# Value products of two units issued as one burst: second batch, first tokens, of an attention + MLP kernel

## The chip, the cores and the metric

The kernel runs on one core of a Trainium2 chip. The time is the device time of one launch in microseconds (us), taken as the median of several runs. Less is better.

## The reference

For 8 batches of 8 heads, 576 positions and head size 64, the reference computes causal windowed attention: heads 0 to 3 see the last 32 keys, heads 4 to 7 see every fourth of the last 128 keys ("dilated"). The result, laid out as 4608 tokens by 512 features, goes through a two-layer MLP:

```
scores = where(mask, q @ k.T / sqrt(64), -1e9)
attn   = exp(scores - max); attn = attn / (sum(attn) + 1e-9)
x      = (attn @ v) as (4608, 512)
h      = x @ w_in                # 512 -> 2048
out    = max(0.01 * h, h) @ w_out   # 2048 -> 512
```

All inputs and the output are float32; the kernel computes in fp16 and accumulates in float32.

## The kernel before

**Tiling.** Batches are taken in pairs, `m = b // 2`. Each batch has four *visits*, in the order `hp` = 2, 3, 0, 1: a visit is a pair of heads (2 and 3 are dilated, 0 and 1 plain). Batches 0 and 1 (`b < EARLY`) are cut in two parts. Part 0 takes 384 of the 576 positions in two units, `u` = 0 and 1; part 1 takes the rest in one unit. So part 0 of batch 1 is four visits of two units each.

**One unit** (function `unit`) is this chain. TensorE: scores of 128 keys against 384 query columns into the PSUM bank `sps` (L666 adds a bias that does the masking, L685 multiplies). ScalarE: the exponential into `ee` (L691). TensorE: value products into a PSUM bank `ops`. ScalarE: logarithm (L761) and then exponential with scale -1 (L763) of the sums, which gives their reciprocal in `rc`. VectorE: the product `ops * rc` into `xt` (L767), the normalisation. In part 0 of batches 0 and 1 (`TILED`) the value products are *half-width*: six matmuls per unit whose outputs have 64 partitions, 0 to 63 for one head of the pair and 64 to 127 for the other; four (L729) multiply by values, two (L717) by ones, for the sums.

**Buffers.** For this part there are two `ops` banks and one `sps` bank, given out in rings (`ring`), unit after unit. A unit's value products wait (`o_old`) for the normalisation of the unit that had the bank two units ago. `ee` has four buffers, `rc` three.

**The MLP.** Positions are taken in chunks of 384. For each chunk, `up` makes 16 groups of four matmuls with `w_in` (L792, 128 x 384, banks `hps`), ScalarE applies the leaky ReLU (L803), and `down` multiplies with `w_out` in three tiles of four *parts* of four matmuls each (L841, 128 x 512, banks `fps`); VectorE copies a finished tile out (L851). Chunk 0 is part 0 of batch 0, chunk 1 is part 0 of batch 1. Each `up` of chunk 1 needs the normalisations of all four visits of part 0 of batch 1 (`x_done[1, 0]`); the last visit, `hp` = 1, comes last. A tile of `down` needs one of two `fps` banks, so the third tile of a chunk starts when the first is copied out. The part p of `down` also needs its four slices of `w_out`, which are loaded and cast during this stage.

**What sets the order.** `_Plan.add` collects tasks with an engine, an assumed duration and latency, dependencies, a priority (small is urgent) and a `soft` time. `_Plan.run` goes through simulated time and gives each engine that is free a task whose dependencies are done; the order so found is the order of the instructions, and on the chip each engine takes its instructions in this order. Its choice is

```
pick = min(((t.ready + t.soft > at + 1e-9, t.prio, t.n), t)
           for t in could if t.ready <= at + 1e-9)
```

So a task with `soft` 0.4 (scores and value products) that has become ready less than 0.4 us ago yields to every other ready task that has waited long enough, whatever the priorities. The priorities near the change are: scores `first + step*n + 0.1` and values `first + step*n + 0.2` with first 20 and step 2 for part 0 of batch 1 (n counts visits); part 1 from 40; `up` of chunk 1 from 20.8 in steps of 1.3; parts of `down` of chunk 0 from 21.4 in steps of 1.73; the transposes of the last positions (`rest`, L557) 40. The assumed costs are 0.36 us for a unit's half-width value products and 0.25 latency after them; 0.06 + 0.00085 n and 0.1 + 0.00085 n for logarithm and exponential of n = 192 columns, 0.2 latency each; 0.38 and 0.2 latency for the normalisation; 0.865 for a part of `down`; 0.335 for the scores with their bias. Idle gaps that the plan sees are filled with dummy matmuls (L934), but only up to the first part of `down`.

Of the kernel before, what the change touches and what calls it, by code (L numbers as in the profile page):

```python
# [11 lines left out]
AF = mybir.ActivationFunctionType  # L12
ALU = mybir.AluOpType
# [47 lines left out]
class _Plan:  # L61
# [5 lines left out]
    def add(self, eng, dur, lat, deps, fn, prio, soft=0.0, kind=""):  # L67
        choices = eng if isinstance(eng, tuple) else ((eng, dur),)
        t = _Task(choices, lat, deps, fn, prio, soft, len(self.tasks), kind)
        self.tasks.append(t)  # L70
        return t
# [66 lines left out]
def kernel(  # L138
# [10 lines left out]
    nc = tc.nc  # L149
# [12 lines left out]
    EARLY = 2  # L162
# [14 lines left out]
    def at(tl, p0, p1, off, *dims):  # L177

        row = tl.ap[0][0]
        return bass.AP(tensor=tl.tensor, offset=tl.offset + p0 * row + off,  # L180
                       ap=[[row, p1 - p0]] + [list(d) for d in dims])
# [43 lines left out]
    add = plan.add  # L225
# [31 lines left out]
    def ring(name, n, users):  # L257

        r = rings.setdefault(name, [])
        waits = r[-n] if len(r) >= n else []  # L260
        r.append(users)
        return (len(r) - 1) % n, waits
# [39 lines left out]
    def heads_of(b, vi):  # L302
        return (2 * vi, 2 * vi + 1) if b < EARLY else (4 * (vi // 2) + vi % 2,
                                                       4 * (vi // 2) + vi % 2 + 2)
# [155 lines left out]
    def chunk_at(m, x):  # L460
        return next(c for c, (mc, xc, n) in enumerate(chunks) if mc == m and xc <= x < xc + n)

    def pieces(b, hp, u, tiled):


        dil = hp >= 2
        m, res = b // 2, []
        u_lo, u_hi = ((0, 96) if u < 2 else (96, 144)) if dil else (48 * u, 48 * u + 48)
        h0, h1 = heads_of(b, hp)
        xm = xt[m % 2]  # L470
        for u0, nu, base in segs[b]:
            lo, hi = max(u0, u_lo), min(u0 + nu, u_hi)
            if lo >= hi:
                continue
            key = (chunk_at(m, base), b % 2 if b < EARLY and lo >= 96 else 0)
            n = hi - lo
            x = base + lo - u0 + (2 * u * nu if dil and u < 2 else 0)
            xs = [[24, 2], [nu, 4], [1, 24]] if not dil else [[nu, 2 if u < 2 else 4], [1, n]]
            if tiled:
                cs = ([[96, 2], [24, 4], [1, 24]] if not dil else  # L480
                      [[192 // xs[0][1], xs[0][1]], [1, n]])
                res.append((key, 0, 128, at(xm, 0, 128, h0 // 2 * 1152 + x, *xs), 0, cs))
                continue
            step = 192 if not dil or u < 2 else 96
            cs = [[192, 2], [24, 4], [1, 24]] if not dil else [[step, xs[0][1]], [1, n]]
            if dil and b >= EARLY:
                p0 = h0 % 2 * 64
                res.append((key, 0, 64,
                            at(xm, p0, p0 + 64, h0 // 2 * 1152 + x, xs[0], [1152, 2], xs[1]), 0,
                            [cs[0], [step // 2, 2], cs[1]]))  # L490
                continue
            for hh, h in enumerate((h0, h1)):
                p0 = h % 2 * 64
                res.append((key, 0, 64, at(xm, p0, p0 + 64, h // 2 * 1152 + x, *xs),
                            step // 2 * hh, cs))
        return res


    x_done, x_free = {}, {1: w_used[14] + w_used[15]}
    k_turned = []  # L500
    rings["F"] = [[], k_turned]
# [136 lines left out]
    def unit(b, hp, part, u, turned, prio):  # L638
        dil = hp >= 2
        ready, t_users, qb, kb = turned  # L640
        na, c_qk, n_users, vt, v_deps, v_users = visits[b, hp, part]
        m, par = divmod(b, 2)
        tiled = (b, part) in TILED
        sk, ok = ("S0", "O0") if b == 0 and part == 0 else ("S", "O")
        sn, s_old = ring(sk, len(banks[sk]), s_users := [])
        on, o_old = ring(ok, len(banks[ok]), o_users := [])
        en, e_old = ring("E", NE, e_users := [])
        rn, r_old = ring("R", NR, r_users := [])
        st, ot, et, rt = banks[sk][sn], banks[ok][on], ee[en], rc[rn]
# [3 lines left out]
        small = dil and u == 2  # L653
# [3 lines left out]
        def scores(e):  # L657
# [18 lines left out]
            for i in range(2):  # L676
# [5 lines left out]
                else:  # L682
# [9 lines left out]
                                                 scale=SCALE), prio + 0.1)  # L692
        s_users.append(t_e)

        def mask(e):
# [11 lines left out]
        t_m = t_e if by_pe else add(  # L707
            (("DVE", 0.41), ("POOL", 0.95)) if b in POOL_MASK else "DVE", 0.41, 0.15, [t_e, t_con],
            mask, prio + 0.1)

        def values(e):
            if tiled:
                for x in range(5 if small else 3):
                    for hh in range(2):
                        p0 = 64 * hh
                        if x == (4 if small else 2):
                            nc.tensor.matmul(  # L717
                                ot[p0:p0 + 64, 192:384], ones,
                                (at(et, 0, 128, 48 * hh, [96, 4], [1, 48]) if small else
                                 at(et, 0, 128, 96 * hh, [192, 2], [1, 96])),  # L720
                                start=True, stop=True)
                        elif small:
                            nc.tensor.matmul(
                                ot[p0:p0 + 64, 48 * x:48 * x + 48],
                                at(vt, 0, 128, (hh * 8 + x) * 128, [1, D]),
                                et[:, 96 * x + 48 * hh:96 * x + 48 * hh + 48],
                                start=True, stop=True)
                        else:
                            nc.tensor.matmul(  # L729
                                ot[p0:p0 + 64, 96 * x:96 * x + 96],  # L730
                                at(vt, 0, 128, (hh * (8 if dil else 6) + 2 * u + x) * 128, [1, D]),
                                et[:, 192 * x + 96 * hh:192 * x + 96 * hh + 96],
                                start=True, stop=True)
                return
            if small:
                for s in range(4):
                    for hh in range(2):
                        c = 96 * s + 48 * hh
                        nc.tensor.matmul(  # L739
                            ot[:, c:c + 48],  # L740
                            at(vt, 0, 128, (hh * 8 + 4 * (b >= EARLY) + s) * 128, [1, 128]),
                            et[:, c:c + 48], start=True, stop=True)
                return
            for i in range(2):
                t = 2 * u + i
                for hh in range(2):
                    va = at(vt, 0, 128, (hh * (8 if dil else 6) + t) * 128, [1, 128])
                    c = 192 * i + 96 * hh
                    nc.tensor.matmul(ot[:, c:c + 96], va, et[:, c:c + 96],  # L749
                                     start=True, stop=True)  # L750

        t_v = add("PE", 0.36 if tiled else 0.21 if small else 0.17, 0.25, [t_m] + v_deps + o_old,
                  values, prio + 0.2, 0.4, "v")
        e_users.append(t_v)
        v_users.append(t_v)
        if tiled:
            r_in, r_out, n_r = ot[:, 192:384], rt[:, 0:192], 192
        else:
            r_in, r_out, n_r = ot[64:128, 0:384], rt[0:64, :], 384
        t_l = add("ACT", 0.06 + n_r * 0.00085, 0.2, [t_v] + r_old,  # L760
                  lambda e: nc.scalar.activation(out=r_out, in_=r_in, func=AF.Ln), prio + 0.2)  # L761
        t_r = add("ACT", 0.1 + n_r * 0.00085, 0.2, [t_l],
                  lambda e: nc.scalar.activation(out=r_out, in_=r_out, func=AF.Exp, scale=-1.0),  # L763
                  prio + 0.2)
        for key, p0, p1, dst, c, i_ in pieces(b, hp, u, tiled):
            def norm(e, p0=p0, p1=p1, dst=dst, c=c, i_=i_):
                nc.vector.tensor_tensor(out=dst, in0=at(ot, p0, p1, c, *i_),  # L767
                                        in1=at(rt, p0, p1, c, *i_), op=ALU.mult)
            t_n = add("DVE", 0.61 if dil and b >= EARLY else 0.38, 0.2,
                      [t_r] + x_free.get(m, []), norm, prio + 0.2)  # L770
            x_done.setdefault(key, []).append(t_n)
            o_users.append(t_n)
            r_users.append(t_n)


    gt_free = {1 - NG: sum(w_used[11:14], []), 2 - NG: w_used[0] + w_used[1]}
# [208 lines left out]
```

The softmax here doesn't subtract the row's maximum and nothing guards it: scores larger than these inputs give would overflow.

## Time and profile before

| | |
|---|---|
| median of 5 runs | 316.75 us (316.04 to 317.94) |
| the profiled execution | 317.94 us, its span in the profile 316.2 us |
| TensorE (PE) busy | 304.1 us, 96% of the span |
| ScalarE (ACT) busy | 219.4 us, 69% |
| VectorE (DVE) busy | 175.5 us, 56% |
| GpSimd (POOL) busy | 120.1 us, 38% |
| granted TensorE clock | 1.00 |
| value products of part 0 of batch 1 | start 43.15 us, last start 54.55 us |
| first `up` of chunk 1 | starts 56.92 us |

Rows of the groups and of the timeline name a line of the kernel (L792), the engine, the operation, and output and input by the program's names. In the timeline, columns are the start, the length from the first start to the last end, and a count of merged instructions. Ends of matmuls are modelled and overlap the next starts, so differences of starts are used here.

### The profile page before, as it was taken

The page shows a single profiled execution, that of the slowest core. Times are in us where ns is not written, and L with a number is a line of the kernel's source. Part 1 is how long each engine was busy: PE and PEld are TensorE (multiplying, and loading weights), DVE is VectorE, ACT ScalarE, POOL GpSimd, SP SyncE. Part 2 cuts the span into 40 slices and gives each one's busy share as a digit, 9 for nine tenths or more (in the row PEclk, how much of TensorE's full clock was granted, in tenths as well). Part 3 has the DMA queues.
Part 4 walks back from the last instruction along what each step waited for, and adds up shares of the span by engine and source line. Part 5 has one row for each costly group of instructions (what it writes and reads, how often), then busy time and mean ns, then how long its engine had stood idle before and what let it go on. Part 6 is the DMA issues. An engine that isn't in the chain of part 4 may idle for free.

```text
span 316.2 us, 6332 instructions
## 1 busy us (share of the span) xinstructions
PE 304.1 (96%) x2257; PEld 179.5 (57%) x2257; DVE 175.5 (56%) x396; ACT 219.4 (69%) x501; POOL 120.1 (38%) x174
## 2 busy tenths in 40 slices
PE   7858899999999999999999999999999999999995
PEld 3525554667777666655555555555555555555544
DVE  5855985647897776876758767664343421000011
ACT  3826585689898999988788888788787843333310
POOL 4457655382684545837628456450000000000000
PEclk9999999999999999999999999999999999999999
DMA  7999998999999899889989979711111111211113
GB/s 245 279 343 403 401 332 172 245 165 220 229 185 190 150 253 188 162 208 218 188 200 191 194 178 184 171 35 33 35 33 35 33 35 36 56 42 35 33 33 100
DMA packets 158175, 51.14 MB, mean 162 GB/s; under 512 B 139200, under 2 KB 151616, under 8 KB 158144
## 3 DMA queue, kind: packets, MB, share of 16 engines
q1 hardware_dynamic: 157696, 50.46, 67.1%
q10 hardware_dynamic: 448, 0.29, 0.4%
q8 instruction: 17, 0.28, 0.4%
q14 instruction: 14, 0.11, 0.1%
HBM read 41.30 MB, written 9.44 MB: 160 GB/s over the span
## 4 chain that ended last, share of the span: by engine, by line
PE 86%; DMA 4%; SPq 3%; DVE 3%; ACT 2%; issue 1%; POOL 0%; POOLq 0%
PE fps L841 39%; PE hps L792 37%; PE sps L685 4%; PE ops L749 3%; SPq L239 3%; DMA stg<-in_k_dram 2%; DMA stg<-in_q_dram 2%; DVE slots L509 1%; PE tp L557 1%; PE ops L739 1%; ACT gt L803 1%; PE sps L669 1%; DVE nat L249 1%; ACT rc L761 0%; PE sps L666 0%
## 5 line engine op out<-in xcount | busy, mean ns | idle before, releaser
L792 PE MATMUL hps<-xt,w_in 128*128 128x384 f16 (+1 forms) x824 | 149.9, 314 | 3.5 <-DVE w_in L249 1.4
L841 PE MATMUL fps<-w_out,gt 128*128 128x512 f16 (+1 forms) x592 | 145.7, 373 | 0.0
L803 ACT ACTIVATE gt<-hps 128x384 f16<-128x384 f32 (+1 forms) x206 | 93.9, 462 | 50.9 <-PE hps L792 46.9
L792 PEld LDWEIGHTS <-w_in 128*128 128x128 f16 x832 | 75.9, 98 | 46.8 <-DVE w_in L249 2.9
L841 PEld LDWEIGHTS <-gt 128*128 128x128 f16 x592 | 55.7, 98 | 45.1
L767 DVE TENSOR_TENSOR xt<-ops,rc 64x192 f16<-64x192 f32 (+2 forms) x138 | 52.3, 398 | 37.2 <-ACT rc L763 36.1
L544 POOL COPY slots<-turned 64x576 f16<-64x576 f16 x48 | 34.7, 723 | 59.8 <-DVE turned L539 57.3
L851 DVE COPY osb<-fps 128x512 f32<-128x512 f32 (+1 forms) x37 | 24.8, 670 | 55.7 <-PE fps L841 55.3
L705 DVE TENSOR_TENSOR ee<-ee,con 128x384 f16<-128x384 f16 x78 | 38.4, 495 | 30.5 <-ACT ee L691 29.8
L761 ACT ACTIVATE rc<-ops 64x384 f32<-64x384 f32 (+1 forms) x94 | 43.2, 463 | 14.5 <-PE ops L717 4.8
L691 ACT ACTIVATE ee<-sps 128x384 f16<-128x384 f32 x92 | 44.7, 486 | 10.3 <-PE sps L685 8.0
L763 ACT ACTIVATE rc<-rc 64x384 f32<-64x384 f32 (+1 forms) x96 | 46.8, 492 | 1.4
L249 POOL CAST nat<-stg 128x576 f16<-128x576 f32 (+1 forms) x52 | 35.0, 695 | 5.8 <-DMA stg<-in_k_dram 2.3
L685 PE MATMUL sps<-slots 128*128 128x192 f16 x152 | 25.0, 246 | 0.5 <-DVE slots L509 0.4
L685 PEld LDWEIGHTS <-slots 128*128 128x128 f16 x160 | 15.8, 102 | 11.7 <-DVE slots L509 0.8
L249 POOL CAST vd<-vst 128x1024 f16<-128x1024 f32 (+2 forms) x20 | 17.5, 897 | 6.3 <-DMA vst<-in_v_dram 6.1
L550 DVE STREAM_TRANSPOSE slots<-nat 128x576 f16<-128x576 f16 x24 | 18.0, 762 | 1.3 <-POOL nat L249 1.1
L539 DVE STREAM_TRANSPOSE turned<-nat 128x576 f16<-128x576 f16 x24 | 18.1, 763 | 0.1
L509 DVE COPY slots<-tp 64x128 f16<-64x128 f16 (+5 forms) x47 | 14.4, 319 | 4.8 <-PE tp L557 4.2
L749 PEld LDWEIGHTS <-vp 128*128 128x128 f16 x160 | 11.1, 98 | 5.6
L249 POOL CAST vp<-vst 128x768 f16<-128x768 f32 x16 | 12.9, 823 | 3.2 <-DMA vst<-in_v_dram 1.8
L749 PE MATMUL ops<-ee,vp 128*128 128x96 f16 x160 | 13.3, 206 | 0.0
(64 smaller groups left out, 132.6 us busy)
## 6 DMA issues: line engine op xcount, KB each, us to landing
vst<-in_v_dram SPq DMA_DIRECT2D x14, 512.0 KB, 5.1
stg<-in_q_dram SPq DMA_DIRECT2D x48, 144.0 KB, 4.1
stg<-in_k_dram SPq DMA_DIRECT2D x48, 144.0 KB, 3.0
vst<-in_v_dram SPq DMA_DIRECT2D x6, 768.0 KB, 5.7
out_dram<-osb SPq DMA_DIRECT2D x16, 192.0 KB, 2.3
gt<-in_moe_w_in_dram SPq DMA_DIRECT2D x5, 512.0 KB, 7.1
out_dram<-osb SPq DMA_DIRECT2D x24, 96.0 KB, 2.1
out_dram<-osb SPq DMA_DIRECT2D x14, 128.0 KB, 2.7
```

What stands on the lines that cost most here:

```text
L249: ENG[e].tensor_copy(out=dst, in_=src)
L544: lambda e, p0=p0, hh=hh: nc.gpsimd.tensor_copy(out=at(qb, p0, p0 + 64, hh * S + o, *od), in_=at(xb, p0, p0 + 64, i, *id_)), prio)
L685: nc.tensor.matmul(st[:, 192 * i:192 * i + 192], ka, qa, start=not by_pe, stop=i == 1 or not by_pe)
L691: lambda e: nc.scalar.activation(out=et, in_=st[:, 0:384], func=AF.Exp, scale=SCALE), prio + 0.1)
L705: ENG[e].tensor_tensor(out=io, in0=io, in1=mk, op=ALU.mult)
L749: nc.tensor.matmul(ot[:, c:c + 96], va, et[:, c:c + 96], start=True, stop=True)
L761: lambda e: nc.scalar.activation(out=r_out, in_=r_in, func=AF.Ln), prio + 0.2)
L763: lambda e: nc.scalar.activation(out=r_out, in_=r_out, func=AF.Exp, scale=-1.0),
L767: nc.vector.tensor_tensor(out=dst, in0=at(ot, p0, p1, c, *i_), in1=at(rt, p0, p1, c, *i_), op=ALU.mult)
L792: nc.tensor.matmul(ht[:, 0:n], at(w_in, 0, 128, i * DFF + j // 2 * 256 + j % 2, [2, 128]), at(xt[m % 2], 0, 128, i * 1152 + x0 + x, [1, n] ...
L803: lambda e: nc.scalar.activation(out=gt[c % NG][:, j * n_c + x:j * n_c + x + n], in_=ht[:, 0:n], func=AF.Prelu, alpha=0.01),
L841: nc.tensor.matmul(ft[:, 0:n_o], g[:, j * n_c + tt * 128:j * n_c + tt * 128 + 128], w_out[:, j * DM + c0:j * DM + c0 + n_o], start=(j == 0 ...
```

## The change

In part 0 of batch 1 (`(b, part) == (1, 0)`) the value task of the first unit of a visit isn't added when the unit is built. What it needs, its matmuls and its successors (logarithm, exponential, normalisations) are kept in `half_visit`. When the second unit is built, one task is added that needs what both need and issues the six matmuls of the first unit and then the six of the second. Its assumed cost is 0.53 us, in place of twice 0.36. The successors of both units depend on it. All other parts of the kernel are added as before; since the order is planned anew, instructions after this can change places.

```diff
+    half_visit = []
...
-        t_v = add("PE", 0.36 if tiled else 0.21 if small else 0.17, 0.25, [t_m] + v_deps + o_old,
-                  values, prio + 0.2, 0.4, "v")
-        e_users.append(t_v)
-        v_users.append(t_v)
...
+        need = [t_m] + v_deps + o_old
+
+        def finish(t_v):
+            e_users.append(t_v)
+            v_users.append(t_v)
...
+        if (b, part) != (1, 0):
+            finish(add("PE", 0.36 if tiled else 0.21 if small else 0.17, 0.25, need, values,
+                       prio + 0.2, 0.4, "v"))
+        elif u == 0:
+            half_visit.append((need, values, finish))
         else:
...
+            need_0, values_0, finish_0 = half_visit.pop()
+
+            def both(e):
+                values_0(e)
+                values(e)
+            t_both = add("PE", 0.53, 0.25, need_0 + need, both, prio + 0.2, 0.4, "v")
+            finish_0(t_both)
+            finish(t_both)
```

The body of `finish` (logarithm, exponential, normalisations) is the old code, indented.

More of the change, by code (lines that the diff above doesn't have):

```diff
@@ L750, in values @@
                                      start=True, stop=True)
-        t_v = add("PE", 0.36 if tiled else 0.21 if small else 0.17, 0.25, [t_m] + v_deps + o_old,
-                  values, prio + 0.2, 0.4, "v")
-        e_users.append(t_v)
-        v_users.append(t_v)
-        if tiled:
-            r_in, r_out, n_r = ot[:, 192:384], rt[:, 0:192], 192
-        else:
-            r_in, r_out, n_r = ot[64:128, 0:384], rt[0:64, :], 384
-        t_l = add("ACT", 0.06 + n_r * 0.00085, 0.2, [t_v] + r_old,
-                  lambda e: nc.scalar.activation(out=r_out, in_=r_in, func=AF.Ln), prio + 0.2)
@@ L762, in unit @@
[L762 to L773, printed above, removed]
+        need = [t_m] + v_deps + o_old
@@ new lines, in finish, with norm @@
+        def finish(t_v):
+            e_users.append(t_v)
+            v_users.append(t_v)
+            if tiled:
+                r_in, r_out, n_r = ot[:, 192:384], rt[:, 0:192], 192
+            else:
+                r_in, r_out, n_r = ot[64:128, 0:384], rt[0:64, :], 384
+            t_l = add("ACT", 0.06 + n_r * 0.00085, 0.2, [t_v] + r_old,
+                      lambda e: nc.scalar.activation(out=r_out, in_=r_in, func=AF.Ln), prio + 0.2)
+            t_r = add("ACT", 0.1 + n_r * 0.00085, 0.2, [t_l],
+                      lambda e: nc.scalar.activation(out=r_out, in_=r_out, func=AF.Exp, scale=-1.0),
+                      prio + 0.2)
+            for key, p0, p1, dst, c, i_ in pieces(b, hp, u, tiled):
+                def norm(e, p0=p0, p1=p1, dst=dst, c=c, i_=i_):
+                    nc.vector.tensor_tensor(out=dst, in0=at(ot, p0, p1, c, *i_),
+                                            in1=at(rt, p0, p1, c, *i_), op=ALU.mult)
+                t_n = add("DVE", 0.61 if dil and b >= EARLY else 0.38, 0.2,
+                          [t_r] + x_free.get(m, []), norm, prio + 0.2)
+                x_done.setdefault(key, []).append(t_n)
+                o_users.append(t_n)
+                r_users.append(t_n)
```

## The prediction

> **What bounds the kernel now.** I read the page first (busy shares and slices), then the table by stage, then the timeline of TensorE around the change, then that of ScalarE and VectorE at its end.
>
> ```profile
> PE 304.1 (96%) x2257; PEld 179.5 (57%) x2257; DVE 175.5 (56%) x396; ACT 219.4 (69%) x501; POOL 120.1 (38%) x174
> PE   7858899999999999999999999999999999999995
> PE 86%; DMA 4%; SPq 3%; DVE 3%; ACT 2%; issue 1%; POOL 0%; POOLq 0%
> ```
>
> TensorE is full from about 40 us to the end, and makes up 86% of the chain that ended last. A TensorE us saved after 40 us is a us of the kernel, if nothing else comes to be late. The table by stage (length, then busy time of each engine, PE first) says the same of the stretch with the value products:
>
> ```profile
> 43.15:54.73 11.58, 11.58 (x104) 5.91 (x103) 8.05 (x21) 6.54 (x21) 6.15 (x9) 1.00 0.91 203
> 54.73:56.92 2.19, 2.19 (x19) 1.24 (x17) 1.27 (x5) 1.00 (x4) 0.93 (x2) 1.00 0.91 173
> ```
>
> TensorE is never idle; VectorE is busy for 8.05 of 11.58 us and ScalarE for 6.54. Now TensorE in order of time:
>
> ```profile
> 47.39 1.03 PE L841 MATMUL fps<-w_out,gt 128*128 128x512 f16 x4
> 48.35 0.28 PE L729 MATMUL ops<-ee,vd 128*64 128x96 f16 x4
> 48.46 0.25 PE L717 MATMUL ops<-ee,ones 128*64 128x192 f16 x2
> 48.64 1.04 PE L841 MATMUL fps<-w_out,gt 128*128 128x512 f16 x4
> ...
> 49.84 1.89 PE L841 MATMUL fps<-w_out,gt 128*128 128x512 f16 x8
> 51.66 0.28 PE L729 MATMUL ops<-ee,vp 128*64 128x96 f16 x4
> 51.77 0.25 PE L717 MATMUL ops<-ee,ones 128*64 128x192 f16 x2
> 51.85 0.25 PE L729 MATMUL ops<-ee,vp 128*64 128x96 f16 x4
> 51.94 0.25 PE L717 MATMUL ops<-ee,ones 128*64 128x192 f16 x2
> 52.12 0.34 PE L666 MATMUL sps<-con 128*128 128x384 f16 x1
> ```
>
> The first four lines are one unit alone; the last six are two units that already stand together. The same rows at 43.15, 44.73 and 46.76 are alone, those at 54.28 together. So **two of the four visits (the plain ones) are already the burst that the change asks for**; only the dilated two can gain.
>
> [...] an L841 matmul takes 0.216 us of a stream (8 in 1.73 us in the chain), so four from 47.39 would let the next begin at 48.25; the half-width group begins at 48.35. About 0.10 us is lost at entry, and at the exit the last L717 start is 0.18 before the next full-width one. [...] two units' products occupy TensorE for half a us, and their logarithms, exponentials and normalisations end 1.85 us after the first matmul (below). [...] four L729 together take 0.28 us, while one takes 0.21.
>
> **The change part by part.**
>
> [...] A unit alone costs 48.64 - 48.25 = 0.39 us of TensorE. Two together: the eight L841 from 49.84 would end at 51.565, and 52.12 - 51.565 = 0.555. Each dilated visit saves 2 x 0.39 - 0.555 = 0.225 us, both 0.45 us. No matmul goes or comes. This alone moves the first `up` of chunk 1 from 56.92 to 56.47.
>
> *Added: the first unit waits for the second.* The burst waits for the second unit's exponential, and for both `ops` banks. Behind it in TensorE's queue stand scores and `down` parts. Overlap of one unit's evacuation with the next's products is given up. I work this out with the planner's costs, because they set the order. Unfused, products to free bank: 0.36 + 0.25 + 0.223 + 0.2 + 0.263 + 0.2 + 0.38 + 0.2 = 2.08. Fused, counting two logarithms, two exponentials and two normalisations in turn: 0.53 + 0.25 = 0.78; the second logarithm ends at 1.23, the exponentials at 1.49 and 1.75, the normalisations at 2.07 and 2.45; with 0.2 the second bank is free at 2.65. With `soft` 0.4 a burst is preferred 3.05 us after the one before, and it must then wait for a `down` part in progress to end (0.865 us each, so 0.4 on average).
>
> *Where the bursts land.* The first needs the bank whose normalisation runs 43.31 to 44.02. With 0.2 and 0.4 that is 44.62; TensorE, after the next scores and one `down` part, is free at about 44.35 and takes another part, so the burst stands at about 45.2 (before, the pair stood at 43.15 and 44.73). Three links of 3.05 put the last burst at 54.4 at the earliest, and with three waits of 0.4 at 55.6. Before, the last pair stood at 54.28.
>
> *What is late next.* Behind the last pair stood exactly this filler, and then the first `up`, which needs the last normalisation:
>
> ```profile
> 54.28 0.28 PE L729 MATMUL ops<-ee,vp 128*64 128x96 f16 x4
> ...
> 54.73 1.04 PE L841 MATMUL fps<-w_out,gt 128*128 128x512 f16 x4
> 55.61 0.61 PE L557 MATMUL tp<-con,rest 128*128 128x128 f16 x8
> ```
>
> ```profile
> 55.51 0.62 DVE L767 TENSOR_TENSOR xt<-ops,rc 128x192 f16<-128x192 f32 x2 [1.30 <-ACT rc L763]
> 56.26 1.38 DVE L509 COPY slots<-tp 64x128 f16<-64x128 f16 x5
> ```
>
> and a last `down` part from 56.06 to 56.92. The normalisations end at 56.13, which is 54.28 + 1.85; with 0.1 for the signal (estimate: L761 starts 0.04 us after its matmuls, at 52.06, so 0.04 to 0.2) `up` could start at 56.23, and starts at 56.92. **The cover is 0.69 us.** All twelve `down` parts of chunk 0 are used up by then: parts started at 33.45, 34.54, 43.77, 45.81, 47.39, 48.64, two from 49.84, two from 52.46, 54.73 and 56.06. If the last burst slips behind more of them, nothing is left to cover its evacuation. With 56.47 as the end of all TensorE work ahead of `up`, the start of `up` by what still lies behind the last burst (0.555 itself, transposes 0.45, a part 0.865):
>
> - transposes and one part or more: burst at 54.60, `up` at 56.55 or, with two parts, at 56.47: **-0.37 to -0.45 us**.
> - one part: burst at 55.05, `up` at 57.00: +0.08.
> - the transposes only: burst at 55.46, `up` at 57.41: +0.49.
> - nothing: burst at 55.91, `up` at 57.86: +0.94.
>
> My placing (54.4 to 55.6, somewhat late in that) falls among the lower three; I take the middle one, **+0.49 us**.
>
> *What costs nothing.* ScalarE and VectorE do the same instructions; in 43 to 57 us they have 5 and 3.5 us idle, and the links in the trace (3.3 us and more from pair to pair) are longer than the evacuation. `ee` and `rc` are held longer by half a us: an exponential comes four units after its buffer's last, covered by the same idle time; if not, scores wait, and that is in the upper bound. No DMA is added. GpSimd's casts of values end at 49.5, before the bursts that need them; SP's loads are not passed by anything. The work after 57 us is planned anew, about half a us later or earlier. The trace shows no price for that: I bound it between -0.3 us (the stalls that TensorE still has near 112 us, up to 0.3) and +0.8 us (one new wait as long as a `down` part), and take 0.
>
> *Sum.* -0.45 saved, +0.94 waited: +0.49. The profiled execution took 317.94 us, its span 316.2, so 1.7 lie around it; it would become 318.4, its span 316.7. It was the slowest of the five; against the median of 316.75 the forecast is 317.2 us.
>
> **The rivals.**
>
> *The cover holds (a gain).* If the first burst is taken at 44.4 already, or slots happen to fall well, the last burst keeps the transposes and a part behind it: -0.37 to -0.45, 316.3 us. For it: in the trace each link has about a us to spare on the chip (1.85 of evacuation in 2.62 us from 51.66 to 54.28). Against it: the order is set by the planner's longer 2.65 + 0.4.
>
> *The last burst comes last of all (slower).* The transposes and all twelve parts go ahead of it and `up` stands bare behind the evacuation: +0.94 us, and if scores of part 1, whose operands come through the copies L509 (1.38 us of VectorE from 56.26), are put ahead of `up`, up to 0.3 us more: 317.7 to 318.0. It decides when the planner has the last burst ready only after about 55.5. For it: three waits of 0.4 lead to 55.6. Against it: the waits can be shorter than average, and scores or transposes give finer slots than parts.
>
> *The new plan loses elsewhere.* A wait appears after 60 us, where ScalarE is busy for 9.60 of 10 us (70 to 80 us): +0.8 or more on top of any of these, 318 us and above. Against it: TensorE is full to the end, so other work is mostly there to fill in.
>
> *Little changes, since half the bursts exist already.* This is inside the sum: without it the gain would have been 0.9.
>
> **How the numbers follow.** Forecast (one part or the transposes behind, 316.8 to 317.3): 0.42. Cover holds: 0.30. Last of all: 0.20. Loss elsewhere: 0.08. About 0.3%, 0.95 us, is what a measurement of this kernel can tell from no change. The first two cases lie within it; of the third about three quarters lie above 317.7, of the fourth nearly all; a gain past 0.95 us needs luck in the later plan as well. That gives 0.05 faster, 0.70 same, 0.25 slower. The range: the gain of 0.45 and 0.2 of scatter below, 316.1; the last-of-all case above, 318.1.
>
> **What would show it.** Right: four bursts L729 x4, L717 x2, L729 x4, L717 x2, the dilated ones saving 0.225 us each; the first burst near 45 us; the last about 1 us later in the order than before, with a part or the transposes behind it; and an idle gap of 0.5 to 1.4 us before the first L792 of chunk 1. Wrong: no gap there and that L792 at 56.5 (the cover holds), or the gap made up by other work, or waits of TensorE before 54 us on the second `ops` bank, or new ones after 60 us.

## The result and the profile after

The change made the kernel slower: median 318.15 us (29 runs) against 316.94 us (50 runs of the kernel before), ratio 1.0043, 95% interval 1.0026 to 1.0060, or +1.4 us (+0.8 to +1.9) of the time before; the two medians differ by 1.2 us, inside this interval. The forecast was 317.2 us with a range to 318.1. The measured time is just past its end, and the order on TensorE is the one of the rival "the last burst comes last of all".

The two profiled executions have the same span, 316.2 us, and would hide this. So I read both traces from one common point. Up to the scores of the second unit of part 0 of batch 1 (the L666 at 39.41 us before the change, called the *anchor*) the order on TensorE is the same in both, and the time to it differs: 39.41 us before, with TensorE busy for 31.17 of it, and 38.27 after, with 30.34. From the anchor to the start of the last matmul it is 272.75 us before and 273.90 after: **+1.15 us**. Line numbers after the change are a little higher: L809 is the `up` that was L792, L858 the `down` part (L841), L730 and L718 the value products (L729, L717), L670 the scores of part 1 (L669), L769 the normalisation (L767), L868 the tile copy (L851), L510 the copies of transposed tiles out of `tp` (L509), L692 the exponential of scores (L691). In the kernels of the experiments they differ by a few again.

The page of the changed kernel, the rows that answer to those of before:

```profile
PE 302.8 (96%) x2257; PEld 179.3 (57%) x2257; DVE 174.0 (55%) x397; ACT 219.0 (69%) x501; POOL 119.1 (38%) x173
PE   7868999899999999999999999999999999999995
PE 88%; DMA 4%; SPq 3%; DVE 3%; ACT 1%; issue 0%; POOL 0%
```

In the slice that starts at 55.3 us, TensorE has fallen from 9 to 8. The table by stage, cut at the end of the last burst and at the first `up`:

```profile
42.00:55.30 13.30, 13.30 (x120) 7.12 (x118) 9.08 (x25) 6.18 (x21) 7.77 (x11) 1.00 0.94 217
55.30:57.28 1.98, 0.60 (x12) 0.40 (x9) 1.87 (x8) 1.51 (x5) 0.09 (x1) 1.00 0.75 199
```

Through all four bursts TensorE is full. Then, in 1.98 us, it works for 0.60. The waits of TensorE from 42 us to the end name what it waits for:

```profile
PE sps L670 <- DVE slots L510: 0.8, 1, 0.8
PE sps L670 <- ACT ee L692: 0.6, 1, 0.6
PE ops L750 <- DVE ee L706: 0.3, 1, 0.3
```

And in order of time:

```profile
53.91 1.03 PE L858 MATMUL fps<-w_out,gt 128*128 128x512 f16 x4
54.86 0.28 PE L730 MATMUL ops<-ee,vp 128*64 128x96 f16 x4
54.97 0.25 PE L718 MATMUL ops<-ee,ones 128*64 128x192 f16 x2
55.05 0.25 PE L730 MATMUL ops<-ee,vp 128*64 128x96 f16 x4
55.14 0.25 PE L718 MATMUL ops<-ee,ones 128*64 128x192 f16 x2
56.19 0.34 PE L670 MATMUL sps<-slots 128*128 128x96 f16 x4 [0.81 <-DVE slots L510]
57.12 0.33 PE L670 MATMUL sps<-slots 128*128 128x96 f16 x4 [0.58 <-ACT ee L692]
57.28 0.57 PE L809 MATMUL hps<-xt,w_in 128*128 128x384 f16 x2
```

The last burst stands behind the last part of `down` and the transposes. Nothing is left to do but the scores of part 1, and these wait too: 0.81 us for copies on VectorE and, since there is one `sps` bank, 0.58 us for an exponential. The second matmul of `up` starts at 57.54 us, 2.68 us after the burst, where 1.95 us had been worked out. VectorE shows why the first `up` comes as late as it does:

```profile
55.69 1.14 DVE L510 COPY slots<-tp 64x128 f16<-64x128 f16 x5
56.86 0.62 DVE L769 TENSOR_TENSOR xt<-ops,rc 128x192 f16<-128x192 f32 x2
```

The copies of the last positions go ahead of the last visit's normalisations. These begin 2.00 us after the burst; before the change they began 1.23 us after the last pair (54.28 and 55.51 us), so they are 0.77 us late.

The loss arises wholly ahead of this point. From the second matmul of `up` to the last matmul it is 255.07 us before and 254.63 after, and 0.34 of the difference are the two groups of scores that are done earlier.

### The profile page after: what moved, and what is told of

Same layout as the page of the kernel before. It is cut to its first block, busy times and chain, and to the rows that moved or that the text cites. A ratio compares the mean times of both kernels' runs of the same rounds, so it can differ in the third digit from the quotient of the medians.

```text
span 316.2 us, 6333 instructions
## 1 busy us (share of the span) xinstructions
PE 302.8 (96%) x2257; PEld 179.3 (57%) x2257; DVE 174.0 (55%) x397; ACT 219.0 (69%) x501; POOL 119.1 (38%) x173
## 4 chain that ended last, share of the span: by engine, by line
PE 88%; DMA 4%; SPq 3%; DVE 3%; ACT 1%; issue 0%; POOL 0%
PE fps L858 39%; PE hps L809 38%; PE sps L686 4%; PE ops L750 3%; DMA wst<-in_moe_w_in_dram 3%; SPq L239 3%; DVE slots L510 1%; DMA stg<-in_k_dram 1%; PE ops L740 1%; PE tp L558 1%; PE sps L670 1%; DVE ee L706 1%; PE sps L667 0%; DVE nat L249 0%; DVE osb L868 0%
## 5 line engine op out<-in xcount | busy, mean ns | idle before, releaser
L809 PE MATMUL hps<-xt,w_in 128*128 128x384 f16 (+1 forms) x824 | 150.4, 314 | 2.9 <-DVE w_in L249 1.6
L858 PE MATMUL fps<-w_out,gt 128*128 128x512 f16 (+1 forms) x592 | 145.7, 373 | 0.0
L809 PEld LDWEIGHTS <-w_in 128*128 128x128 f16 x832 | 76.0, 98 | 46.2 <-DVE w_in L249 2.3
L858 PEld LDWEIGHTS <-gt 128*128 128x128 f16 x592 | 55.6, 98 | 45.4
L769 DVE TENSOR_TENSOR xt<-ops,rc 64x192 f16<-64x192 f32 (+2 forms) x138 | 51.7, 397 | 39.2 <-ACT rc L765 38.2
L868 DVE COPY osb<-fps 128x512 f32<-128x512 f32 (+1 forms) x37 | 24.8, 670 | 56.9 <-PE fps L858 56.6
L692 ACT ACTIVATE ee<-sps 128x384 f16<-128x384 f32 x92 | 44.7, 486 | 13.6 <-PE sps L686 11.8
L510 DVE COPY slots<-tp 64x128 f16<-64x128 f16 (+5 forms) x47 | 14.4, 319 | 4.9 <-PE tp L558 4.2
L750 PEld LDWEIGHTS <-vp 128*128 128x128 f16 x160 | 11.0, 98 | 5.1
L750 PE MATMUL ops<-ee,vp 128*128 128x96 f16 x160 | 13.3, 206 | 0.0
```

What stands on the lines that cost most here:

```text
L692: lambda e: nc.scalar.activation(out=et, in_=st[:, 0:384], func=AF.Exp, scale=SCALE), prio + 0.1)
L750: nc.tensor.matmul(ot[:, c:c + 96], va, et[:, c:c + 96], start=True, stop=True)
L809: nc.tensor.matmul(ht[:, 0:n], at(w_in, 0, 128, i * DFF + j // 2 * 256 + j % 2, [2, 128]), at(xt[m % 2], 0, 128, i * 1152 + x0 + x, [1, n] ...
L858: nc.tensor.matmul(ft[:, 0:n_o], g[:, j * n_c + tt * 128:j * n_c + tt * 128 + 128], w_out[:, j * DM + c0:j * DM + c0 + n_o], start=(j == 0 ...
```

## The experiments

The theory: the saving of the two dilated bursts (0.45 us by the prediction's sum) is real, and the loss is the evacuation of a last burst that the planner has put behind all the work that covered it before (theory 1). *Evacuation* is the way from the burst to the last normalisation, *cover* the work that TensorE has meanwhile. Rivals: bursts cost in themselves, or the plan after 60 us is worse (theory 2); and, for a part of the loss, that a gap on TensorE makes the chip grant it a lower clock (theory 3; 14 of 29 executions of the change had a mean clock below 0.997, with a median of 319.6 us against 317.7 for the others).

All ratios are to the kernel before, timed on the same chip in the same stretch. "First `up`" is the start of its second matmul, since the first doesn't read the last visit's heads. Both times in us are differences of starts from the anchor in the profiled execution; up to the anchor the order on TensorE is the same in all twelve kernels. The granted clock behind it is 1.00 in the profiles of before and of the change, and in every stretch from 40 us of soft0 and fill. The mean over the whole execution is 1.00 for moved, plain, pinned, soft2 and hold, 0.999 for dil0, 0.998 for copies and 0.994 for cover.

| kernel | behind the last burst | ratio (95%) | first `up` | last matmul | against before |
|---|---|---|---|---|---|
| before | two parts, transposes | 1 | 17.68 | 272.75 | |
| the change | nothing | 1.0043 (1.0026 to 1.0060) | 19.27 | 273.90 | +1.15 |
| soft0 | two parts, transposes | 0.9985 (0.9965 to 1.0004) | 17.23 | 272.25 | -0.50 |
| moved | nothing | 1.0037 (1.0019 to 1.0056) | 18.96 | 274.02 | +1.27 |
| fill | nothing (dummies) | 1.0045 (1.0022 to 1.0068) | 19.27 | 273.90 | +1.15 |
| plain | one part | 1.0043 (1.0023 to 1.0063) | 19.27 | 273.89 | +1.14 |
| pinned | two parts, transposes | 0.9990 (0.9969 to 1.0011) | 17.22 | 272.34 | -0.41 |
| dil0 | two parts, transposes | 1.0002 (0.9985 to 1.0019) | 17.22 | 272.66 | -0.09 |
| soft2 | one part | 1.0038 (1.0020 to 1.0056) | 18.80 | 274.10 | +1.35 |
| hold | one part | 1.0033 (1.0011 to 1.0054) | 18.53 | 274.02 | +1.27 |
| copies | one part | 1.0034 (1.0018 to 1.0051) | 18.81 | 274.07 | +1.32 |
| cover | two parts | 0.9992 (0.9964 to 1.0020) | 17.23 | 272.53 | -0.22 |

**soft0: the change with the bursts taken earlier.**

```diff
-            t_both = add("PE", 0.53, 0.25, need_0 + need, both, prio + 0.2, 0.4, "v")
+            t_both = add("PE", 0.53, 0.25, need_0 + need, both, prio + 0.2, 0.0, "v")
```

> The change, with soft time 0.0 in place of 0.4 on the four bursts, so that the planner takes each burst 2.65 us after the one before and no longer 3.05. By the planned order the last burst then has two parts of down and the transposes of the last positions behind it, as the last pair had before. Theory 1 (the loss is the bare evacuation of a last burst that comes last of all): the 1.38 us of idle TensorE ahead of the first up are gone, [...]: about 0.998 to 0.999 of the kernel before, against 1.0043 for the change. Theory 2 (bursts cost, or the plan after 60 us is worse): about 1.004 again.

Measured: 0.9985, and 272.25 us from the anchor. TensorE of this kernel at the same place:

```profile
54.03 0.28 PE L730 MATMUL ops<-ee,vp 128*64 128x96 f16 x4
54.14 0.25 PE L718 MATMUL ops<-ee,ones 128*64 128x192 f16 x2
54.22 0.25 PE L730 MATMUL ops<-ee,vp 128*64 128x96 f16 x4
54.31 0.25 PE L718 MATMUL ops<-ee,ones 128*64 128x192 f16 x2
54.49 1.04 PE L858 MATMUL fps<-w_out,gt 128*128 128x512 f16 x4
55.36 0.61 PE L558 MATMUL tp<-con,rest 128*128 128x128 f16 x8
55.81 1.03 PE L858 MATMUL fps<-w_out,gt 128*128 128x512 f16 x4
56.67 0.65 PE L809 MATMUL hps<-xt,w_in 128*128 128x384 f16 x3
```

The same four bursts as in the change, with the filler behind the last one and no wait. The first `up` starts 0.45 us earlier than before, the full saving. The loss is not in the bursts.

**moved: the loss without a burst.** In the finished order of the kernel before, the last visit's value products and their successors go to just ahead of the first `up` (`last_visit` collects these tasks, `ups_1` the `up` tasks of chunk 1, in lines left out here):

```diff
...
     order = plan.run()
+    late = sorted(last_visit, key=lambda t: (t.start, t.n))
+    for i, t in enumerate(late):
+        t.start = min(u.start for u in ups_1) - 0.01 + 0.0005 * i
+    order.sort(key=lambda t: (t.start, t.n))
```

> The kernel before, without any burst; alone the value products of the last visit of part 0 of batch 1, with their logarithms, exponentials and normalisations, are moved in the order to just ahead of the first up of chunk 1. All else keeps its order. Theory 1: the evacuation is bare, 1.85 + 0.1 - 0.555 = 1.4 us of idle TensorE, so about 1.0044 of before without any burst. Theory 2: no loss, 1.000. If idle TensorE also lowers the granted clock in part of the executions (theory 3), more than 1.0044 and clocks below 0.997 in some executions.

Measured: 1.0037, +1.27 us from the anchor. The trace has one wait there, in the middle of the first `up`:

```profile
55.26 0.25 PE L718 MATMUL ops<-ee,ones 128*64 128x192 f16 x2
55.44 0.34 PE L797 MATMUL hps<-xt,w_in 128*128 128x384 f16 x1
56.89 0.81 PE L797 MATMUL hps<-xt,w_in 128*128 128x384 f16 x4 [1.12 <-DVE xt L769]
```

From the start of the pair at 54.98 to the release is 1.91 us, against 1.95 expected. Position alone costs 1.27 us, without any burst. The change loses 1.15 after a saving of 0.45, so 1.60 in all; the rest is taken up below.

**fill: dummies in the gap.**

```diff
                 values_0(e)
                 values(e)
+                for _ in range(3 * (hp == 1)):
+                    nc.tensor.matmul(hps[0], warm[:, 0:128], warm, start=True, stop=True)
...
+                for _ in range(2 * (b == 1 and part == 1 and hp == 2)):
+                    nc.tensor.matmul(hps[0], warm[:, 0:128], warm, start=True, stop=True)
```

> The change, with five dummy matmuls of 128 x 512 in the two waits ahead of the first up: three behind the last burst, two behind the first scores of part 1; the order is otherwise the same. They add no work where TensorE would wait anyway (0.8 and 0.6 us). Theory 1 alone: as the change, 1.004. Theory 3 (the idle gap makes the chip grant a lower clock in about half of the executions, which costs these 1.7 us): granted clock 0.997 or more in nearly all executions and about 1.002 to 1.003 of before.

Measured: 1.0045, as the change; theory 3 got nothing. The gap is filled:

```profile
56.85 0.82 PE L791 MATMUL hps<-warm 128*128 128x512 f16 x3
57.72 0.34 PE L670 MATMUL sps<-slots 128*128 128x96 f16 x4
57.90 0.59 PE L677 MATMUL hps<-warm 128*128 128x512 f16 x2
```

The granted clock of this very execution was 0.993 all the same. The table by stage (the clock is the third number from the end) shows where it was lost:

```profile
20.00:25.00 5.00, 3.00 (x13) 1.49 (x14) 2.27 (x10) 1.21 (x4) 3.94 (x6) 0.81 1.05 369
25.00:30.00 5.00, 4.89 (x35) 2.64 (x32) 2.47 (x9) 2.77 (x7) 3.75 (x7) 0.85 1.05 415
55.00:60.00 5.00, 4.80 (x45) 2.52 (x44) 4.65 (x19) 2.34 (x8) 0.00 (x0) 1.00 0.76 159
```

It was lost at 20 to 30 us, ahead of everything that the change touches; at 55 to 60 us it is 1.00. A clock below 0.997 was seen in 14 of 29 executions of the change, in 10 of 22 of fill, with its gap filled, and in 19 of 75 of the kernel before; but also in 10 of 22 of pinned, which has no gap, and in only 5 of 22 of moved, which has one. Nor does the loss hang on such executions: among the others the median is 317.53 us for fill and 317.86 for moved, against 316.35 for the kernel before.

**plain: bursts only where pairs stood already.**

```diff
-        if (b, part) != (1, 0):
+        if (b, part) != (1, 0) or dil:
```

> Bursts only in the two plain visits, whose pairs stood together before already: [...] only the dependency on both units and the assumed cost differ. In the planned order the last burst has one part of down behind it in place of two and the transposes, and the scores of part 1 go ahead of the first up. Theory 1: evacuation 1.95 less burst 0.555 less part 0.865 leaves a wait of about 0.5 us, up to 1 with the copies of part 1: 1.0015 to 1.003. Theory 2 (the bursts themselves cost): the plain two should cost nothing, since their matmuls stood together already: 1.000.

Measured: 1.0043, above the 1.0015 to 1.003 expected, with no burst that wasn't a pair before. Only the planner's view differs: it has the last burst one part and the transposes later, and then puts the scores of part 1 ahead of `up`:

```profile
54.92 1.04 PE L858 MATMUL fps<-w_out,gt 128*128 128x512 f16 x4
55.79 0.33 PE L670 MATMUL sps<-slots 128*128 128x96 f16 x4
56.70 0.33 PE L670 MATMUL sps<-slots 128*128 128x96 f16 x4 [0.58 <-ACT ee L692]
56.87 0.33 PE L809 MATMUL hps<-xt,w_in 128*128 128x384 f16 x1
57.54 0.32 PE L809 MATMUL hps<-xt,w_in 128*128 128x384 f16 x1 [0.34 <-DVE xt L769]
```

So one part of cover is not worth what I had taken it for (0.865 us). Later runs (soft2, hold, copies, cover) take this up.

**pinned: the bursts without a new plan.** The kernel before, planned as before; in the finished order the first unit's tasks of the two dilated visits move next to the second's (`firsts` and `seconds` hold, by visit, the value products, logarithm, exponential and list of normalisations of each, in lines left out here):

```diff
...
     order = plan.run()
+    for hp in (2, 3):
+        for x, y in zip(firsts[hp][:3], seconds[hp][:3]):
+            x.start = y.start - 0.0001
+        for x in firsts[hp][3]:
+            x.start = max(x.start, seconds[hp][3][0].start - 0.0001)
+    order.sort(key=lambda t: (t.start, t.n))
```

> The kernel before, planned as before; only in the finished order the first unit's value products of the two dilated visits, with their logarithm, exponential and normalisation, are moved next to the second unit's. So there are the four bursts of the change, and no new plan. If [...] the loss of the change is its plan alone: two visits save 0.225 us each and the cover of 0.69 us holds, 272.75 - 0.45 = 272.3 us from the scores of the second unit (the anchor) to the last matmul, 0.9986 of before. If bursts cost in themselves (both banks taken at once, evacuation in pairs): 1.000 or more.

Measured: 272.34 us from the anchor, -0.41 (-0.45 expected), first `up` 0.45 earlier. The ratio 0.9990 agrees, but its interval includes 1.

**dil0: bursts in the dilated visits, soft time 0.** The condition is `(b, part) != (1, 0) or not dil`, the soft time 0.0.

> Bursts in the two dilated visits alone, with soft time 0; the plain visits' value products are planned unit by unit as before. By the order all four visits come out in pairs, and two parts of down and the transposes lie behind the last one. Same as the run with soft 0 on all four, if what matters is where the last pair lies: 0.9985, 272.25 us from the anchor to the last matmul. If the planned dependency on both units in the plain visits matters too, it differs from that by some tenths of a us.

Measured: the first `up` is 0.45 us earlier, as with soft0, but the end only 0.09 and the ratio 1.0002. The waits of this kernel after 60 us say where the rest went:

```profile
PE hps L809 <- ACT gt L820: 0.6, 2, 0.4
```

Two waits for the leaky ReLU on ScalarE, at 111 and 115 us, which soft0 doesn't have. This is what a new plan can cost after the place of the change: 0.4 us here.

**soft2: half the soft time.** As soft0, with 0.2.

> The change with soft time 0.2 in place of 0.4. By the order the last burst has one part of down behind it (none with 0.4, two and the transposes with 0), and the scores of part 1 still go ahead of the first up. Between the two: the run with bursts in the plain visits has the same end and lost 1.14 us without any saving, so 1.14 - 0.45 = +0.7 us here, 1.002 of before. If only the loss of all cover decided, it would be near 0.9985; if the later plan decided, near 1.004.

Measured: 1.0038, +1.35 us: a miss. Going by the first `up` the rule "+1.14 - 0.45" was nearly right: 18.80 is 1.12 late, and `plain` 1.59. To this the end adds a wait of 0.6 us: at 119 us in this kernel's order, scores wait for a transpose on VectorE. Why the first `up` is late with a part behind the burst (at 53.36 us) shows on VectorE:

```profile
52.60 2.53 DVE L510 COPY slots<-tp 64x128 f16<-64x128 f16 x12 [0.45 <-PE tp L558]
55.16 0.69 DVE L868 COPY osb<-fps 128x512 f32<-128x512 f32 x1
55.77 0.61 DVE L769 TENSOR_TENSOR xt<-ops,rc 128x192 f16<-128x192 f32 x2
```

The copies of the last positions and the copy of the tile that the part finishes both go ahead of the normalisations, which begin 2.41 us after the burst in place of 1.23. The next runs take these two apart.

**hold: normalisations ahead of the copies of the last positions.** As soft2, and

```diff
-                                        [tq] + zq + zk + (busy if dil and o else []), prio))
+                                        [tq] + zq + zk + (busy if dil and o else [])
+                                        + (x_done[1, 0] if b == 1 else []), prio))
```

> The run with soft time 0.2, and the copies L510 of the last positions (part 1 of batch 1) depend in addition on the normalisations of part 0. So VectorE does the last visit's normalisations first, and TensorE the first up ahead of the scores of part 1; one part of down still lies behind the last burst. If the evacuation alone sets the first up: last burst at 15.73 us after the anchor, plus 1.95, first up at 17.68 against 17.51 before, a wait of 0.53, and an end later by 0.17 us, 1.0005 of before. If the copies and scores that went ahead cost nothing: as with soft time 0.2, 1.12 to 1.35 us later, 1.0038.

Measured: 1.0033 and 18.53: another miss, and the most useful one. The scores are out of the way, yet TensorE waits 1.15 us in the first `up`:

```profile
58.11 0.32 PE L810 MATMUL hps<-xt,w_in 128*128 128x384 f16 x1 [1.15 <-DVE xt L770]
```

VectorE:

```profile
53.74 0.35 DVE L770 TENSOR_TENSOR xt<-ops,rc 128x192 f16<-128x192 f32 x1
56.84 0.69 DVE L869 COPY osb<-fps 128x512 f32<-128x512 f32 x1 [2.74 <-PE fps L859]
57.44 0.61 DVE L770 TENSOR_TENSOR xt<-ops,rc 128x192 f16<-128x192 f32 x2
```

The last part of `down` finishes a tile, and the copy of that tile stands ahead of the last normalisations in VectorE's queue. VectorE idles 2.74 us for it, and `up` starts 2.81 us after the burst of 55.30 us, where 1.95 had been worked out. So the work that was to cover the evacuation holds it up.

**copies: the change, with the tile copies less urgent.** In `down`, the priority `-1000 if c else 30.0` in place of -1000; soft time 0.4 as in the change.

> The change with soft time 0.4 kept, but VectorE's copies of the tiles of down of chunk 0 (L868) get priority 30 in place of -1000, so the planner puts normalisations of part 0 ahead of them where both are ready. By the order the last burst moves from behind all parts to ahead of the last one, as with soft time 0.2. If those copies delay the third burst and with it the last: about 15.7 us from the anchor to the last burst in place of 16.6, a third link shorter than 4.67 us, and the time as with soft time 0.2, 1.003 to 1.004. If they don't matter: 16.6 us and 1.0043.

Measured: as expected. The third burst follows the second by 3.48 us in place of 4.67 (46.93 to 50.41), the last stands 15.73 us after the anchor, and time and first `up` (18.81) are those of soft2. Shortening the link alone doesn't bring the time back.

**cover: both.** As hold, and the tile copies at priority 30.

> The run hold (soft time 0.2, copies of the last positions after the last normalisations) with, in addition, priority 30 in place of -1000 for VectorE's copies of the tiles of down of chunk 0, so they no longer go ahead of the last visit's normalisations. By the order two parts of down lie behind the last burst and the first up is ahead of the scores of part 1. Two parts are 1.73 us, the burst 0.555, together more than the evacuation of 1.95: no wait, first up 17.06 us after the anchor, end 0.45 us earlier than before apart from the later plan, 0.9986. If something other than the bare evacuation held the first up back in the run hold (18.53 us to its second matmul), that stays, and 1.003 with it.

Measured: 0.9992; first `up` at 17.23, no wait before it. VectorE now has the last normalisations ahead of the tile copy:

```profile
55.72 0.62 DVE L770 TENSOR_TENSOR xt<-ops,rc 128x192 f16<-128x192 f32 x2 [2.35 <-ACT rc L766]
56.88 0.69 DVE L869 COPY osb<-fps 128x512 f32<-128x512 f32 x1 [0.42 <-PE fps L859]
```

With soft time 0.2 and bursts as in the change, the loss is gone once two parts lie behind the last burst and its normalisations are first in VectorE's queue. No run separates these two conditions. The end is -0.22: 0.3 us go to a wait for ScalarE at 143 us, as in dil0.

Of the versions here soft0 and pinned are the best, -0.5 and -0.4 us by their traces. Their intervals reach past 1, so a gain over the kernel before is not shown by the times; that they beat the change is (0.9985 and 0.9990 against 1.0043, with intervals that don't meet).

## Why the prediction was wrong, step by step

*What bounds the kernel, and the saving: right.* In the trace of the change the first dilated burst takes 0.54 us of TensorE (44.52 less 42.25 and eight L858 of 0.216), for 0.555 worked out and 2 x 0.39 for two units alone. With the cover in place the first `up` starts 0.45 us earlier in soft0, pinned and dil0, for 0.45 worked out. Two of four visits had nothing to gain, as the trace of before showed.

*The cover and the price of a bare last burst: right.* `moved` measures 1.91 us from burst to `up`, for 1.95, and loses 1.27 us, for 0.94 + 0.45 = 1.39 without the saving. The list of prices takes the first matmul of `up` for the one that waits; it is the second, 0.16 us later, so the list is high by about that much.

*Where the bursts land: the first step that failed.* The first was put at 45.2 us of the clock of before; it came at 44.07 + 1.14 = 45.2. The last was put at 54.4 to 55.6, with 55.5 as the point from which nothing is left behind it; it came at 54.86 + 1.14 = 56.0. The links were 3.39, 4.67 and 2.73 us, for 3.05 and an average wait of 0.4. The second is the one I mis-sized: my chain of one link had ScalarE and VectorE free, but the copies of two finished tiles go ahead of the normalisations:

```profile
48.99 0.69 DVE L868 COPY osb<-fps 128x512 f32<-128x512 f32 x1 [0.35 <-PE fps L858]
49.60 0.34 DVE L769 TENSOR_TENSOR xt<-ops,rc 128x192 f16<-128x192 f32 x1
49.86 0.68 DVE L868 COPY osb<-fps 128x512 f32<-128x512 f32 x1
50.46 0.35 DVE L769 TENSOR_TENSOR xt<-ops,rc 128x192 f16<-128x192 f32 x1
```

`copies` confirms it: with those copies less urgent the link is 3.48 us. I had read VectorE's 8.05 us of 11.58 as room; what counted was who stands ahead in its queue. The two normalisations took 0.34 and 0.35 us and ended 3.35 us after the start of their burst (50.81 and 47.46), where those of the first burst ended 1.85 us after its start (45.92 and 44.07): this evacuation was late by its place in VectorE's queue, and not by its own work. So the last burst had nothing behind it, where I had taken the transposes: +0.94 in place of +0.49 by my own list, 0.45 of the 0.66 us by which the trace (+1.15) lies above the forecast. The rival "last of all" had this order.

*What the last burst waits for: the second step that failed.* The list counts what lies behind the burst on TensorE and puts VectorE's queue at nothing. In the change, the copies of the last positions stand there and make the normalisations 0.77 us late. The parts of the loss up to the second matmul of `up`: -0.45 saved, +1.28 for the bare position (as in `moved`), +0.77 for these copies; together 1.60, and 1.59 measured. Of this 0.34 is not lost, since scores are done in the wait, which leaves 1.25. For one part behind the burst the list says +0.08; soft2, hold and copies have one part there and lose 1.3 us. A part that ends a tile brings a tile copy, and the planner uses the time to bring scores and copies of part 1 forward; on VectorE both stand ahead of the normalisations in soft2 and copies, the tile copy alone in hold. I counted the part's time on TensorE and not what it issues on VectorE. So with the link sized rightly and this list, the forecast would have been further off.

*Work after 60 us: within the bounds given.* The change has one new wait of 0.3 us there (L750, at 155.6 us), and some small gaps of before are gone (one of 0.26 us near 112 us, three of 0.11 to 0.15); in all it gains 0.1 us after the first `up`, and so ends at +1.15. In dil0 the new plan costs 0.4. The measured +1.4 and the trace's +1.15 agree within the interval. That the time is just past the end of the range and not just inside it is chance: the base was 316.75 us from five runs, and 316.94 from fifty.

*Two readings of the trace of before were wrong.* The shortest link from pair to pair is 2.62 us (51.66 to 54.28), not 3.3, and the 5 and 3.5 us in which ScalarE and VectorE are idle belong to 43 to 55 us, not to 57. No sum rests on them.

## What to carry to other kernels

When two tasks become one, the later one sets when both start and the sum of both sets when their successors end; look first at what the last of them was covered by, and count that cover in each queue that its successors pass, not just on the bound engine. A gain of 0.45 us on the bound engine was real, and 1.60 us were lost against it, because a planner's slack (0.4 us) and two urgent copies moved the last burst behind the work that hid it. And compare traces from a common point past a start whose length varies (39.41 and 38.27 us here): equal spans of 316.2 us hid the whole loss here.

## What the runs showed of the hardware that I had not expected

The granted clock of TensorE falls below 1 in part of the executions of every kernel here, the one before too: 19 of 75 runs timed beside soft0 had a mean clock below 0.997, and a median of 317.76 us against 316.35 for the others. Three of the twelve profiled executions lie below 0.997: soft0 (0.995), fill (0.993) and cover (0.994). In fill the clock is 0.81 at 20 to 25 us and 0.85 at 25 to 30 (the table by stage under fill); in soft0 it is lost in the same two stretches:

```profile
20.00:25.00 5.00, 3.48 (x15) 1.65 (x16) 2.38 (x10) 1.64 (x4) 3.68 (x6) 0.78 1.04 341
25.00:30.00 5.00, 4.50 (x33) 2.59 (x32) 2.85 (x9) 2.69 (x6) 3.48 (x6) 0.88 1.05 413
```

In every other stretch of the two executions it is 1.00. At 20 to 25 us TensorE is busy for 3.00 (fill) and 3.48 (soft0) of 5 us. This does not tell them apart from executions that kept their clock: in the profile of before it is busy for 2.58 us there, in that of the change for 2.93, and the clock is 1.00 in both. No run here varied this, so the cause isn't shown. The waits of the change near 56 us (0.81 and 0.58 us) left the clock at 1.00.
